# Token counts in full 128-column weight blocks, and an experts' planner that knows of exposed weight loads

## The chip, the cores and the metric

The kernel runs on one core of a Trainium2 chip. The metric is the time of one execution on the device in microseconds (us), the median of three runs. A profiled execution of the same kernel gives the trace from which all rows below are taken; times in it count from its first instruction. The engines are PE (TensorE, its weight loads shown apart as PEld), DVE (VectorE), ACT (ScalarE), POOL (GpSimd) and SP, which here only issues DMAs.

## What is computed

```python
attn_out = softmax(q @ pooled(k).T / 8) @ pooled(v)    # 8 x 8 heads, 576 tokens, width 64
x = attn_out.transpose(0, 2, 1, 3).reshape(4608, 512)
# mixture of 8 experts, each takes exactly 576 tokens (cap)
flat = (x @ w_gate).flatten()
for idx in np.argsort(-flat):            # best (token, expert) pairs first
    tok, e = idx // 8, idx % 8
    if assigned[tok] >= 0 or counts[e] >= cap: continue
    assigned[tok] = e; counts[e] += 1
for e in range(8):
    out[assigned == e] = np.maximum(x[assigned == e] @ w1[e], 0) @ w2[e]
# gated feed-forward over all tokens
y = (sigmoid(out @ w_gate2) * (out @ w_val)) @ w_out   # 512 -> 1536 -> 512
```

## The kernel before

There are three stages. Attention and the logits of the gate take the first 155 us of the profile. Then come the experts, and last the gated feed-forward, whose loads and splits begin under the experts' last steps.

**The choice of the tokens.** The greedy loop is replaced by eight rounds, k = 0 to 7. In a round each token that is still free has a key, its best open logit, in two parts `kh` and `kl`. The round must find the key at which the first expert is full. `search` (L898) does it twice, by 16 bits of the key each time, in four steps of four bits, so a round makes eight counts (the last round makes none). For one count DVE compares all keys with 15 thresholds into `C` (128 partitions x 36 token columns x 32, of which 15 are used), PE multiplies `C` as weights with `EoU` (which expert each token wants) and adds up in PSUM (`rps`, in round 0 `acc0`), DVE compares the count with the free places (`hit`, with `fl` as its sum), and PE multiplies `fl` with a table `trw`, which gives the next 15 thresholds. Each of these four links waits for the one before it. In round 0 a matmul takes one token column of 15 thresholds, so a count is 36 matmuls, and one more (`one16` with `nrem`) subtracts the 576 places. In rounds 1 to 6 a matmul takes three token columns, 79 weight columns (3 x 32, less the 17 unused of the last) against 24 of `EoU`, so a count is 12 matmuls; DVE then adds the three diagonal blocks in `jk`, by one subtraction of `rem` and two additions.

After the eight counts a round goes on with `EG` and `tot` (which expert is full), then `est`, the expert's number. From there SP may load that expert's weights (`load`, L1062: four of 1 MB into `stg`); in this document that moment is "the expert is chosen". Then `before`, `inc`, `OHH`, `OHL` and `R` make the list `idxs` of the 576 tokens (36 matmuls `rps<-R,OHL`), after which POOL gathers the tokens' rows by indirect DMAs (`xg`), and the round is "done".

**The experts.** Expert k is computed in two halves of 288 tokens (u), each in eight steps f, so 128 steps of 24 products: 12 for `hps` (g_h, L1198) and 12 for `acc` (g_o, two steps behind). The products are float32 split in a high and a low part: `xh`, `xl`, `hh`, `hl` and the weights `w`, split from `stg` by ACT (high) and DVE or POOL (low). DVE makes `hl` and `xl` from PSUM after ACT has made `hh` and `xh`. The gathered tokens are turned by PE (`hps<-identf,xg`, three transposes to a `turn`, four turns to a half). DVE and ACT also convert the last stage's weights (`cx`, `cs`, `cw`), 36 tiles of four DVE instructions.

**What sets the order.** Rounds 1 to 7 run between the products of earlier experts. `experts` (L1048) is a planner in Python that issues instructions while `Clock` (L634) models the time of each engine; `note` (L678) has the cost of each instruction, 0.039 us for a small matmul with over 64 weight columns. Between groups of three products, `groups` comes back to the loop at L1290: `fill` (L1182) puts in turns, splits and conversions whose data are ready and whose engine is free by the model, and `route` (L1119) goes one link on in the round when that link's data are ready by the model or will be before the next products can run. Every instruction goes through one helper, so that nearly all rows of the experts show L628.

Of the kernel before, what the change touches and what calls it, by code (L numbers as in the profile page):

```python
# [8 lines left out]
F32R = mybir.dt.float32r  # L9
# [4 lines left out]
OP = mybir.AluOpType  # L14
# [8 lines left out]
CAP = N // E  # L23
F1 = 1024
F2 = 1536
NT = N // 128
# [607 lines left out]
class Clock:  # L634
    HOP = 0.15

    def __init__(self, nc):
        self.nc = nc
        self.t = {n: 0.0 for n in ("tensor", "vector", "scalar", "gpsimd", "sync", "dma")}
        for n in ("tensor", "vector", "scalar", "gpsimd", "sync"):  # L640
            setattr(self, n, Lane(self, getattr(nc, n), n))
        self.spans, self.rings, self.free = {}, {}, {}
        self.held = {"vector": deque(maxlen=64), "gpsimd": deque(maxlen=64)}
# [34 lines left out]
    def note(self, lane, op, args, kw):  # L678
# [5 lines left out]
        t = self.t  # L684
# [10 lines left out]
        if "dma" in op:  # L695
            big = max([a.nbytes() for a in aps], default=0)
            t[lane] = start + (1.03 if lane == "gpsimd" else 0.5)
            first = max(t["dma"], t[lane] + 0.8)
            t["dma"] = first + big / 360e3
            end = t["dma"] + 1.0  # L700
        else:
            if lane == "tensor":
                n = aps[-1].free_size() if op == "matmul" else aps[1].partition_size() * 2
                n *= 4 if op == "matmul" and aps[-1].dtype == F32 else 1
                cost = max(0.039 if op == "matmul" and aps[1].free_size() > 64 else 0.0245, n / 2400 + 0.013)
            elif lane == "vector":
                wide = op == "tensor_tensor" and all(mybir.dt.size(a.dtype) == 2 for a in aps)
                cost = 0.069 + n / (1920 if wide else 960)
            elif lane == "scalar":
                cost = 0.07 + n / 1200  # L710
            elif lane == "gpsimd":
                cost = 0.15 + n * 0.0021
            else:
                cost = 0.3
            end = t[lane] = start + cost
            if alone:
                self.held[lane].append((start, end))
# [10 lines left out]
class Router:  # L728
# [168 lines left out]

    def search(self, k, key, w):  # L898
        nc, C, EoU = self.nc, self.C, self.EoU
        g, parts = (1, 3) if k == 0 else (3, 1)  # L900
        TR = self.tr0[:, w]
        for i in range(4):
            if i or w:
                for c in range(0, NT, NT // parts):
                    cs = slice(c, c + NT // parts)
                    nc.vector.tensor_tensor(C[:, cs, 0:15], key[:, cs, None].to_broadcast([128, NT // parts, 15]),
                                            TR[:, None, :].to_broadcast([128, NT // parts, 15]), op=OP.is_ge)
                yield 0.8 / g, (C[:, 0:NT // parts],)
            if k:
                cp = self.psum.tile([32 * g, g, E], F32, name="rps", bufs=1)  # L910
            else:
                cp = self.spare.tile([128, UA], F32, name="acc0", bufs=1)[0:32, 0:E].rearrange("p (g e) -> p g e", g=1)
            for c in range(NT // g):
                nc.tensor.matmul(cp[0:32 * g - 17], C[:, g * c:g * c + g].rearrange("p c t -> p (c t)")[:, 0:32 * g - 17],
                                 EoU[:, g * c:g * c + g], start=c == 0, stop=c == NT // g - 1, skip_group_check=True)
                if c == 0 and not k:
                    nc.tensor.matmul(cp[0:15, 0], self.one16[:, 0:15], self.nrem, start=False, stop=False, skip_group_check=True)
            hits = cp[0:15, 0]
            if k:
                hits = self.jk  # L920
# [1 line left out]
                for j in range(g - 1):  # L922
                    nc.vector.tensor_tensor(hits, cp[32 * j:32 * j + 15, j], hits, op=OP.add)
            rows = slice(32 * i, 32 * i + 15)
            nc.vector.tensor_scalar(self.hit[rows], hits, 0.0, None, op0=OP.is_ge, op1=OP.max, accum_out=self.fl[rows])
            yield 0.05, (self.fl,)
            TR = self.psum.tile([128, 15], F32, name="rps", bufs=1)
            nc.tensor.matmul(TR, self.fl.to_broadcast([128, 128]), self.trw[:, w, i], start=True, stop=True)
# [119 lines left out]
def experts(tc, c, w, xio, psum, router, conv, xD, w1, w2, x2D, ahead, spare):  # L1048
    nc = router.nc
    ident = c["ident"]  # L1050
    now = nc.t
    with ExitStack() as ctx:
# [4 lines left out]
        steps = [(k, u, f) for k in range(E) for u in range(2) for f in range(8)]  # L1057
        order = [(half, which) for half in range(2) for which in range(2)]
        splits, turns, lows, banks = deque(), deque(), deque(), []
        st = {"chosen": 0, "phase": 0, "load": 0, "split": 0, "gather": 0, "turn": 0, "h": 0, "o": 0, "gap": False, "ahead": False}  # L1060

        def load(k, half, which):  # L1062
            eng = nc.gpsimd if (k, half) == (0, 1) else nc.sync
# [96 lines left out]
        def do_turn(force=False):  # L1160
            t = turns[0]
            if force or (st["h"] >= 8 * (2 * t[0] + t[1]) - 8 and len(lows) < 3 and nc.idle(banks[-3]) <= now["tensor"] and nc.when([xg[t[0], t[1], 2]]) <= now["tensor"]
                         and now["scalar"] <= now["tensor"] + 0.3):
                do_lows(1)
                turn(*turns.popleft())
                return True
# [15 lines left out]
        def fill():  # L1182
            do_lows()
            late = False
            while st["gap"] and turns and (turns[0][0], turns[0][1], 2) in xg:
                if not do_turn():
                    late = st["h"] >= 8 * (2 * turns[0][0] + turns[0][1]) - 4 and nc.when([xg[turns[0][0], turns[0][1], 2]]) <= now["tensor"] + 1.0
                    break
# [100 lines left out]
        heat(nc.when([xT[0, 0][0][:, 0]]))  # L1289
        for need in groups():  # L1290
            fill()
            while wait["on"] and (wait["ready"] <= now["tensor"] + 0.05 or wait["ready"] < nc.when(need) - 0.1):
                route()
                fill()
        assert not splits and not turns and not lows


# [751 lines left out]
```

## Time and profile before

| | |
|---|---|
| median of 3 runs | 1486.81 us (1486.62 to 1488.14) |
| the profiled execution's own time | 1487.1 us |
| span of its instructions | 1485.4 us |
| PE busy | 1443.0 us, 97% of the span |
| DVE busy | 1199.4 us, 81% |
| ACT, POOL busy | 578.4 and 453.9 us |
[...]

The profiled execution took 1.7 us more than its span, and 0.3 us more than the median. Busy shares are over all stages; below they are read by stage.

### The profile page before, as it was taken

The page shows a single profiled execution, that of the slowest core. Times are in us where ns is not written, and L with a number is a line of the kernel's source. Part 1 is how long each engine was busy: PE and PEld are TensorE (multiplying, and loading weights), DVE is VectorE, ACT ScalarE, POOL GpSimd, SP SyncE. Part 2 cuts the span into 40 slices and gives each one's busy share as a digit, 9 for nine tenths or more (in the row PEclk, how much of TensorE's full clock was granted, in tenths as well). Part 3 has the DMA queues.
Part 4 walks back from the last instruction along what each step waited for, and adds up shares of the span by engine and source line. Part 5 has one row for each costly group of instructions (what it writes and reads, how often), then busy time and mean ns, then how long its engine had stood idle before and what let it go on. Part 6 is the DMA issues. An engine that isn't in the chain of part 4 may idle for free.

```text
span 1485.4 us, 29007 instructions
## 1 busy us (share of the span) xinstructions
PE 1443.0 (97%) x11228; PEld 1323.7 (89%) x11228; DVE 1199.4 (81%) x2590; ACT 578.4 (39%) x1138; POOL 453.9 (31%) x461
## 2 busy tenths in 40 slices
PE   8999699999999999999999999999999999999997
PEld 6888489999999999998888888888888899999996
DVE  6889788988899987578788868888787897887884
ACT  5665143343433434445434333323432233333321
POOL 5682042254334412202234311112211231334221
PEclk9999699999999999999999999999999999999998
DMA  9994346545554776676565664554756377766751
GB/s 334 315 312 134 104 148 204 174 128 205 189 172 147 225 252 199 249 270 236 213 234 183 231 266 177 216 204 173 259 189 243 135 255 270 284 239 243 297 222 70
DMA packets 133130, 319.25 MB, mean 215 GB/s; under 512 B 13724, under 2 KB 55232, under 8 KB 118784
## 3 DMA queue, kind: packets, MB, share of 16 engines
q1 hardware_dynamic: 125428, 295.39, 56.1%
q0 software_dynamic: 6496, 20.98, 4.2%
q8 instruction: 89, 1.46, 0.4%
q10 hardware_dynamic: 1068, 1.03, 0.3%
q14 instruction: 49, 0.40, 0.1%
HBM read 240.42 MB, written 72.89 MB: 211 GB/s over the span
## 4 chain that ended last, share of the span: by engine, by line
PE 84%; DVE 9%; issue 2%; DMA 2%; ACT 1%; POOL 1%; SPq 1%; ACTq 0%; POOLq 0%; DVEq 0%
PE hps L628 12%; PE acc L628 12%; PE pj L1812 11%; PE Yg L1645 7%; PE Yv L1645 7%; PE pj L1859 7%; PE Zg L1645 5%; PE Xg L1645 5%; PE Zv L1645 5%; PE Xv L1645 5%; PE aps L530 2%; PE rps L628 2%; DVE cx L628 1%; PE sps L469 1%; PE qps L505 1%
## 5 line engine op out<-in xcount | busy, mean ns | idle before, releaser
L628 PE MATMUL acc<-hh,w 128*128 128x288 f32 x1024 | 244.9, 304 | 0.0
L628 PE MATMUL hps<-xh,w 128*128 128x288 f32 x1024 | 234.5, 300 | 1.2 <-DVE hl L628 1.1
L628 PEld LDWEIGHTS acc<-hh,w 128*128 128x128 f32 x1024 | 176.3, 189 | 0.2
L628 PEld LDWEIGHTS hps<-xh,w 128*128 128x128 f32 x1024 | 174.1, 188 | 2.3 <-DVE hl L628 1.8
L628 PE MATMUL acc<-hl,w 128*128 128x288 f32 x512 | 151.1, 295 | 0.9 <-DVE hl L628 0.9
L628 PE MATMUL hps<-xl,w 128*128 128x288 f32 x512 | 151.3, 296 | 0.1
L628 ACT ACTIVATE hh<-hps 128x288 fp32r<-128x288 f32 x128 | 52.5, 410 | 234.6 <-PE hps L628 219.4
L628 POOL TENSOR_TENSOR w<-stg,w 128x512 fp32r<-128x512 f32 x76 | 107.9, 1433 | 114.7 <-ACT w L628 108.6
L1829 DVE TENSOR_TENSOR stg<-pj,stg 128x512 f32<-128x512 f32 (+1 forms) x196 | 121.5, 627 | 23.7 <-PE pj L1812 17.7
L1645 PE MATMUL Yg<-w 128*128 128x512 f32 (+1 forms) x540 | 126.4, 369 | 0.0
L1645 PE MATMUL Yv<-w 128*128 128x512 f32 (+1 forms) x540 | 125.6, 367 | 0.0
L1711 ACT ACTIVATE sg<-sg 128x512 f32<-128x512 f32 (+1 forms) x90 | 53.0, 589 | 177.8 <-DVE sg L1682 110.9
L628 POOL DMA_INDIRECT xg<-x_rows,idxs x48 | 46.2, 963 | 223.0 <-PE hps L628 70.9
L1645 PEld LDWEIGHTS Yv<-w 128*128 128x128 f32 x540 | 98.7, 188 | 13.0 <-DVE vc L1681 0.3
L1645 PEld LDWEIGHTS Yg<-w 128*128 128x128 f32 x540 | 95.8, 189 | 11.4
L628 PEld LDWEIGHTS acc<-hl,w 128*128 128x128 f32 x512 | 96.7, 189 | 1.1 <-DVE hl L628 1.1
L628 PEld LDWEIGHTS hps<-xl,w 128*128 128x128 f32 x512 | 96.4, 188 | 0.3 <-DVE xl L628 0.3
L628 ACT ACTIVATE w<-stg 128x512 fp32r<-128x512 f32 (+1 forms) x137 | 80.8, 639 | 35.4 <-DVE capv L628 29.9
L1645 PE MATMUL Xg<-w 128*128 128x512 f32 (+1 forms) x360 | 84.4, 369 | 0.5 <-ACT cw L628 0.5
L1645 PE MATMUL Zg<-w 128*128 128x512 f32 (+1 forms) x360 | 84.4, 369 | 0.2 <-DVE sg L1689 0.2
L1645 PE MATMUL Zv<-w 128*128 128x512 f32 (+1 forms) x360 | 84.2, 369 | 0.0
L1645 PE MATMUL Xv<-w 128*128 128x512 f32 (+1 forms) x360 | 83.6, 367 | 0.0
(326 smaller groups left out, 3264.6 us busy)
## 6 DMA issues: line engine op xcount, KB each, us to landing
w<-w_split SPq DMA_DIRECT2D x84, 1024.0 KB
stg<-in_moe_w_dram SPq DMA_DIRECT2D x30, 1024.0 KB
w_split<-w SPq DMA_DIRECT2D x21, 1024.0 KB
woh<-wo_parts SPq DMA_DIRECT2D x38, 512.0 KB
wr<-wo_parts SPq DMA_DIRECT2D x19, 768.0 KB
kv<-in_k_dram SPq DMA_DIRECT2D x12, 768.0 KB
kv<-in_v_dram SPq DMA_DIRECT2D x12, 768.0 KB
x_cols<-x SPq DMA_DIRECT2D x15, 576.0 KB
```

Of the source, the lines that this page charges most:

```text
L469: eng.matmul(p[cs, r, G * j:G * j + G], t.ap[rs, h % 4, cs], kpT[rs, b if b is not None else 4 * n + 2 * c + r, h], start=True, stop=True)
L505: eng.transpose(p[:z, j], flat[:, a:a + z], ident)
L530: eng.matmul(p[:, a + s:a + s + 2], t[:, j + s], flat[:, x0:x1 + 1:x1 - x0], start=a + s == 0, stop=True, skip_group_check=True)
L628: r = f(*args, **kw)
L1645: eng.matmul(t, W(a, k), X(b, k), start=first and n == 0, stop=n == 5, skip_group_check=True)
L1711: x = fl.op(A, lambda eng: eng.activation(T(g), T(g), AF.Sigmoid), after=[op], rank=rank)
L1812: eng.matmul(self.tile(ps)[:, 256 * i:256 * i + 256], G(a), W(b), start=j < 4 and i == 0 and q == 0, stop=True, skip_group_check=True)
L1829: y = fl.op({"vector": 0.15 + n * 256 / 960}, lambda eng: eng.tensor_tensor(A(), P(), A(), op=OP.add), after=[x, st["acc", u, k, t, d]], r ...
L1859: eng.matmul(self.tile(ps), G(a), W(b), start=n == 0, stop=n == 5)
```

## The change

Three things are edited. In `search`, a matmul of rounds 1 to 6 takes four token columns (128 weight columns against 32 of `EoU`), so a count is nine matmuls, and DVE adds four diagonal blocks (one subtraction, three additions). In round 0 a matmul takes all 32 columns of its token, the comparison is made in four pieces of nine token columns instead of three of twelve, and the places are compared with 576 on DVE instead of being subtracted by a matmul. In `Clock.note`, a product (float32 in one pass, `F32R`) that follows anything else on PE costs 0.083 us more. In the planner, a turn is put off while a round is running, unless the planner is about to go on with that round (`near`) or the turn is nearly due; and from round 3 on a link of the round is issued only when by the model its data have been ready for 0.5 us.

```diff
 class Clock
+        self.big = True
...
                 cost = max(0.039 if op == "matmul" and aps[1].free_size() > 64 else 0.0245, n / 2400 + 0.013)
+                big = op == "matmul" and aps[-1].dtype == F32R
+                if big and not self.big:
+                    cost += 0.083
+                self.big = big
...
 def search(self, k, key, w)
-        g, parts = (1, 3) if k == 0 else (3, 1)
+        g, parts = (1, 4) if k == 0 else (4, 1)
...
-                yield 0.8 / g, (C[:, 0:NT // parts],)
+                yield 0.75 if k == 0 else 0.3, (C[:, 0:NT // parts],)
...
             for c in range(NT // g):
-                nc.tensor.matmul(cp[0:32 * g - 17], C[:, g * c:g * c + g].rearrange("p c t -> p (c t)")[:, 0:32 * g - 17],
+                nc.tensor.matmul(cp[0:32 * g], C[:, g * c:g * c + g].rearrange("p c t -> p (c t)"),
                                  EoU[:, g * c:g * c + g], start=c == 0, stop=c == NT // g - 1, skip_group_check=True)
-                if c == 0 and not k:
-                    nc.tensor.matmul(cp[0:15, 0], self.one16[:, 0:15], self.nrem, start=False, stop=False, skip_group_check=True)
...
-            nc.vector.tensor_scalar(self.hit[rows], hits, 0.0, None, op0=OP.is_ge, op1=OP.max, accum_out=self.fl[rows])
+            nc.vector.tensor_scalar(self.hit[rows], hits, 0.0 if k else float(CAP), None, op0=OP.is_ge, op1=OP.max, accum_out=self.fl[rows])
...
 def fill() in experts
             while st["gap"] and turns and (turns[0][0], turns[0][1], 2) in xg:
+                k, u, i = turns[0]
+                if len(banks) < 3 or wait["on"] and not st["near"] and st["h"] < 8 * (2 * k + u) - 4 + i:
+                    break
                 if not do_turn():
...
 the loop at L1290
-            while wait["on"] and (wait["ready"] <= now["tensor"] + 0.05 or wait["ready"] < nc.when(need) - 0.1):
+            while wait["on"] and (wait["ready"] <= now["tensor"] + (0.05 if st["phase"] < 3 else -0.5) or wait["ready"] < nc.when(need) - 0.1):
+                st["near"] = True
                 route()
                 fill()
+            st["near"] = False
```

The order of the instructions that comes out of it follows from the planner, not from the diff alone. The first place is on PE, in a round that runs under the third expert's steps: the end of a count, and what stands there until the next link (`fl`). Before:

```order
L628 LDWEIGHTS C
L628 MATMUL rps<-EoU,C 79x24
L628 MATMUL hps<-xh,w 128x288
L628 MATMUL hps<-xl,w 128x288
L628 MATMUL hps<-xh,w 128x288 x2
L628 MATMUL hps<-xl,w 128x288
L628 MATMUL hps<-xh,w 128x288
L628 MATMUL acc_6220<-hh,w 128x288
L628 MATMUL acc_6220<-hl,w 128x288
L628 MATMUL acc_6220<-hh,w 128x288
L628 LDWEIGHTS fl
L628 MATMUL rps<-trw,fl 128x15
```

Of the change, at a like place:

```order
L628 LDWEIGHTS C
L628 MATMUL rps<-EoU,C 128x32
L628 MATMUL hps<-identf,xg 128x96 x3
L628 MATMUL acc_6111<-hh,w 128x288
L628 MATMUL acc_6111<-hl,w 128x288
L628 MATMUL acc_6111<-hh,w 128x288
L628 MATMUL hps<-xh,w 128x288
L628 MATMUL hps<-xl,w 128x288
L628 MATMUL hps<-xh,w 128x288 x2
L628 MATMUL hps<-xl,w 128x288
L628 MATMUL hps<-xh,w 128x288 x2
L628 MATMUL hps<-xl,w 128x288
```

The last of nine matmuls instead of twelve is shown; a turn now follows the count at once, and more products (15 instead of 9) stand before the next link. Over the experts' stage the order has 576 count matmuls before and 432 now, the same 3072 products and 180 transposes, and the returns from anything else to a product fall from 158 to 149.

The second place is on DVE, between a count and its threshold in round 1 (`jk` adds the blocks, `hit` decides). Before:

```order
L628 TENSOR_TENSOR C<-kh,rps 128x36x15
L628 TENSOR_TENSOR w<-stg,w 128x512
L628 TENSOR_TENSOR jk<-rps,rem 15x8
L628 TENSOR_TENSOR jk<-rps,jk 15x8 x2
L628 TENSOR_SCALAR hit,fl<-jk 15x8
L628 SCALAR_TENSOR_TENSOR cx<-cw,cx 128x512
```

Of the change:

```order
L628 SCALAR_TENSOR_TENSOR cx<-cs,cx 128x512
L628 SCALAR_TENSOR_TENSOR hl<-hps,hh 128x288
L628 TENSOR_TENSOR xl<-hps,xh 128x288
L628 TENSOR_TENSOR jk<-rps,rem 15x8
L628 TENSOR_TENSOR jk<-rps,jk 15x8 x3
L628 TENSOR_SCALAR hit,fl<-jk 15x8
```

One more addition stands in each of the 48 counts of rounds 1 to 6. The rounds also come to their ends later. By the products ahead of each round's list of tokens, rounds 1 to 7 are done at step 11.8, 23.8, 36.6, 49.4, 62.8, 75.8 and 79.8 before, and at 11.5, 24.6, 40.6, 56.2, 72.2, 86.6 and 90.2 now, while expert k's products begin at step 16k in both. The order of the gated stage is unchanged on PE.

## Rows read from the trace of the kernel before

**Rows 1.** The page's head and first part: busy us, share of span.
```profile
span 1485.4 us, 29007 instructions
```

**Rows 2.** Windows by stage: us, then busy time by engine, PEclk, DMA share, GB/s.
```profile
155.00:195.00 40.00, 28.41 (x441) 17.61 (x441) 26.76 (x126) 6.43 (x13) 6.05 (x6) 0.66 0.41 133
195.00:560.00 365.00, 358.91 (x3337) 349.44 (x3338) 322.98 (x956) 148.58 (x324) 131.97 (x107) 1.00 0.56 185
672.80:1485.40 812.60, 801.28 (x4420) 718.57 (x4419) 644.19 (x984) 274.57 (x480) 208.46 (x184) 1.00 0.60 220
```

**Rows 3.** Waits of PE, 195 to 345 us (rounds 1 to 3): us in total, times, longest.
```profile
PE rps L628 <- DVE C L628: 1.5, 1, 1.5
PE hps L628 <- DMA xg<-x_rows,idxs: 0.6, 1, 0.6
```

**Rows 4.** Waits of PE, 345 to 672.8 us (the later rounds and steps).
```profile
PE hps L628 <- DVE hl L628: 1.5, 4, 0.5
PE rps L628 <- DVE EG L628: 0.9, 1, 0.9
PE acc L628 <- DVE hl L628: 0.9, 1, 0.9
PE rps L628 <- DVE hit L628: 0.4, 1, 0.4
PE rps L628 <- DVE EoU L628: 0.2, 1, 0.2
```

**Rows 5.** Timeline of PE, one count: start us, us, what.
```profile
256.77 0.61 PE L628 MATMUL rps<-EoU,C 128*79 128x24 bf16 x12
257.23 0.38 PE L628 MATMUL acc<-hh,w 128*128 128x288 f32 x1
257.45 0.29 PE L628 MATMUL acc<-hl,w 128*128 128x288 f32 x1
```

**Rows 6.** Timeline of PE, three small matmuls with 128 weight columns.
```profile
283.97 0.20 PE L628 MATMUL rps<-rs,before 128*128 128x1 bf16 x2
284.03 0.16 PE L628 MATMUL rps<-rs,onesb 128*128 128x1 bf16 x1
284.06 0.38 PE L628 MATMUL acc<-hh,w 128*128 128x288 f32 x1
```

**Rows 7.** Weight loads by form, 195 to 510 us: busy us, mean ns.
```profile
L628 PEld LDWEIGHTS <-C 128*79 128x79 bf16 x576 | 29.1, 124 | 3.2 <-DVE C L628 1.7 <-DVE EoU L628 0.4 <-issue 0.2
L628 PEld LDWEIGHTS <-fl 128*128 128x128 bf16 x48 | 4.6, 96 | 3.8 <-DVE hit L628 0.6
```

**Rows 8.** Timeline of round 0, DVE and PE.
```profile
157.31 0.30 DVE L890 TENSOR_TENSOR C<-kh,tr 128x150 bf16<-128x150 f32 x1
...
163.85 0.85 DVE L628 TENSOR_TENSOR C<-kh,rps 128x180 bf16<-128x180 f32 x3 [0.29 <-PE rps L628]
...
164.31 1.02 PE L628 MATMUL acc<-EoU,C 128*15 128x8 bf16 x35
```

**Rows 9.** Timeline of PE, 36 matmuls with 32 weight columns.
```profile
185.08 1.07 PE L628 MATMUL rps<-R,OHL 128*32 128x36 bf16 x36 [0.37 <-DVE OHL L628]
```

**Rows 10.** Timeline of DVE, the additions after a count.
```profile
271.95 0.16 DVE L628 TENSOR_TENSOR jk<-rps,rem 15x8 f32<-15x8 f32 x1
272.14 0.34 DVE L628 TENSOR_TENSOR jk<-rps,jk 15x8 f32<-15x8 f32 x2
```

**Rows 11.** Timeline of DVE and POOL just ahead of the longest wait.
```profile
258.32 3.15 DVE L628 SCALAR_TENSOR_TENSOR cx<-cs,cx 128x512 f32<-128x512 f32 x1
258.36 2.54 POOL L628 TENSOR_TENSOR w<-stg,w 128x512 fp32r<-128x512 f32 x2
```

**Rows 12.** Timeline of round 3: the expert's weights, from choice to first split.
```profile
333.77 0.13 DVE L628 TENSOR_SCALAR est<-m 1x1 int32<-1x1 f32 x1
334.74 2.35 SPq L628 DMA_DIRECT2D stg<-in_moe_w_dram  x4
...
341.12 0.62 ACT L628 ACTIVATE w<-stg 128x512 fp32r<-128x512 f32 x1
```

More of the change, by code (lines that the diff above doesn't have):

```diff
@@ L1059, in experts @@
         splits, turns, lows, banks = deque(), deque(), deque(), []
-        st = {"chosen": 0, "phase": 0, "load": 0, "split": 0, "gather": 0, "turn": 0, "h": 0, "o": 0, "gap": False, "ahead": False}
+        st = {"chosen": 0, "phase": 0, "load": 0, "split": 0, "gather": 0, "turn": 0, "h": 0, "o": 0, "gap": False, "ahead": False, "near": False}
         def load(k, half, which):
```

## The prediction

> **What bounds the kernel now.** I read the page's head first, for the span that the sum is made against: 1485.4 us [rows 1], with 1.7 us around it in the profiled execution (1487.1 us), which is 0.3 us above the median. Then the windows by stage, to see which engine sets each [rows 2]. From 155 to 195 us no engine is full (PE 28 of 40 us) and the granted clock averages 0.66: this is round 0, where DVE and PE wait for each other in turn, so every link counts in full. From 195 to 560 us, where rounds 1 to 7 run under the products, PE is busy 358.9 of 365 us: PE is the bound, and what it is relieved of comes off the time. DVE is next with 323.0 us, 88%. The gated stage has PE busy for 801 of 813 us; its order on PE is untouched, so it starts when the experts end and lasts as long as before. Third, the waits of PE [rows 3, 4]: seven groups, 6.0 us in all, six of them for DVE. That is all that a better order can give by removing waits. The rest of a gain must come from work that PE no longer does.
>
> **The counts of rounds 1 to 6.** Now twelve matmuls with 79 weight columns run from 256.77 to 257.23 us, 0.46 us or 0.038 each [rows 5]. Neither 24 nor 32 moving columns can be what takes that time: three matmuls with one moving column take 0.09 us [rows 6], so it is the loads or the issue. What do nine with 128 columns take? No count with 128 columns is in the trace, so I bound it. From above: the next row in weight columns below it, 79, has 0.038 each, and a load no faster than that gives nine x 0.0385 = 0.35 us. From below: the three with 128 columns [rows 6] take 0.06 for the first two and 0.03 for the third, so nine take about 0.06 + 7 x 0.027 = 0.25 us. I take 0.25, because those rows have the same weight columns and type, and because a load of 128 bf16 columns takes 96 ns against 124 ns for one of 79 [rows 7]: the full block is the faster load, not the slower. Saved: 48 counts x (0.46 - 0.25) = 10.1 us; with the upper bound 48 x (0.46 - 0.35) = 5.3 us.
>
> [...]
>
> **Returns to a product.** The first product after a count shows 0.38 us where the next has 0.29 [rows 5]: its load lies open for 0.09 us. The order has nine returns fewer (158 to 149): 9 x 0.09 = 0.8 us. The turn that now stands behind a count costs the same three transposes as before, and the new 0.083 in the planner's costs is no time by itself; it only moves links.
>
> **Round 0.** Its counts wait for the first piece of the comparison. Three pieces of 180 elements take 0.85 us together and one of 150 alone takes 0.30 [rows 8]; between these, an element costs at most 0.55 / 390 = 0.0014 us. A first piece of 135 instead of 180 should end up to 0.06 us sooner; I take 0.045, seven times (the first count's comparison is made elsewhere): 0.3 us. The last piece still lands before the matmuls reach it: four pieces, at the 0.28 us that each of the three takes, are done by 1.13 us, and the 28th matmul comes some 0.35 + 27 x 0.029 = 1.13 us after the start. One matmul fewer in each of eight counts, at 1.02 / 35 = 0.029 us [rows 8], is 0.2 us. Against it stand 32 instead of 15 weight columns. 36 such matmuls take 1.07 us, 0.030 each [rows 9], the same as 0.029, but rows 8 were taken at a lower clock. From above I bound them by the 0.038 of 79 columns, 36 x 8 x 0.009 = 2.6 us. I take nothing, as 15 and 32 columns come out alike. Round 0: -0.5 us, between -0.5 and +2.1. It is hidden by nothing, since the experts' first products wait for its list.
>
> **DVE's added work.** One more `jk` in each of 48 counts; the next one starts 0.19 us after the one before [rows 10]: 9.1 us in 48 pieces. Its place is 195 to 560 us, where DVE would be busy 323.0 + 9.1 = 332 us of some 354, 94% instead of 88. In a link the addition lengthens the chain by 0.19 us and the shorter count takes 0.21 off, so the threshold comes as early as before. Queued behind it are `hl` and `xl`, for which PE waits already, 2.4 us [rows 4]. How much of the crowding reaches PE no row shows. Below: nothing, as DVE's idle time is still 22 us. Above: half of the 9.1 us, when every second addition pushes an `hl` that is needed at once. I take 2 us, nearer the lower end, because in the 365 us PE waited for `hl` in five places only.
>
> **The planner's order.** From round 3 on a link waits 0.5 us longer by the model. Three waits there are of links [rows 4]: EG 0.9, hit 0.4, EoU 0.2. 0.5 us off each leaves 0.4: -1.1 us. The longest wait (C, 1.5 us) is earlier [rows 3], in round 2, where the rule does not apply. It came from a conversion that took 3.15 us because POOL split weights beside it [rows 11]. The change keeps such pairs, so one like it stays likely. Since a turn is put off and a round takes more products, rounds 3 to 7 are done 4 to 11 steps later, and expert k's weights are asked for later. What covers that: expert 3's four loads are issued at 334.74 us and its first split runs at 341.12, 7.4 us after the choice [rows 12]. In the new order round 3 is done at step 40.6 and is chosen before that, while the products of expert 3 start at step 48. Seven steps of 24 products at 0.13 us (0.22 from the first to the second, less the open 0.09 [rows 5]) are 22 us. I cost it at nothing; the cover is gone once a choice comes some 15 us later than planned, and then each late us is a us of PE.
>
> **The sum.** Counts -10.1, returns -0.8, round 0 -0.5, links' waits -1.1, DVE +2.0: -10.5 us. Against the profiled 1487.1 that gives 1476.6, and against the median, 0.3 lower, **1476.3 us**, a ratio of 0.993.
>
> **The rivals.**
>
> 1. A load of 128 columns in a count is no faster than one of 79 (0.0385 each). For it: the planner's own costs know only one value over 64 columns, and such loads stand only in short runs [rows 6]. Against it: the shorter load [rows 7]. The gain on counts is 5.3 instead of 10.1 us: 1481.1 us.
> 2. DVE gives half of its added work on to PE and the links' waits move instead of going, as `hl` waits: +4.5 instead of +2.0, and 0 instead of -1.1. For it: six of seven wait groups are already for DVE, and at 94% the slack is thin. Against it: DVE has some 42 idle us in the stretch now [rows 2], and PE waited for it 5.4 us in all [rows 3, 4]. 1479.9 us; if all 9.1 us came through, 1484.5.
> 3. Slower: a load takes time in proportion to its columns, 0.0385 x 128 / 79 = 0.062 us. Nine take 0.56 us, 0.10 more than now, +4.8 us on 48 counts, and with the other terms (-0.8, -0.5, -1.1, +2.0) the kernel takes 1491.2 us. It decides as soon as a matmul with 128 columns takes over 0.052 us, where nine equal the present count. Against it stand [rows 6, 7].
> 4. Also slower: the later rounds bring weights or tokens late. It decides when the five experts of rounds 3 to 7 wait together for over 10.5 us, about 2.1 us each; with 4 us each the kernel takes 1476.3 + 20 = 1496.3 us. Against it: the 15 us of cover.
> 5. Nothing comes of it: PE's gain is waited away at the seam to the gated stage, where weights must be there. For it: DMAs are busy 0.60 of the gated stage [rows 2]. Against it: the gated stage's loads are issued by steps, so they move with PE. 1486.8 us.
>
> **How the numbers follow.** A measurement of this kernel tells about 0.2%, 3 us, from no change, so faster is below 1483.8 us. My forecast, 1472 to 1479 us by itself, has 0.62; rival 1 0.13; rival 2 0.14; rivals 3 and 4 together 0.05; rival 5 0.06. Downward the range takes in a planner that removes most of the waits (4 us more than I count), 1472; upward rivals 1 and 2, to 1482.5. Faster: 0.62 + 0.13 + 0.12 = 0.87; same: 0.02 of rival 2 and 0.06 of rival 5, 0.08; slower 0.05.
>
> **What would show it.** In the new profile a count should read x9 with about 0.25 us from its start to the next product; 0.35 there means rival 1, over 0.46 rival 3. Loads of `C` should show some 96 ns instead of 124. The last product of the experts should end near 662 us instead of 672.8. Waits of PE for `hl` and `xl` over 5 us in sum mean rival 2, waits for DMAs or for ACT's `w` at steps 48, 64, 80 or 96 rival 4, a wait ahead of the first gated product of over 1 us rival 5. The prediction is wrong above all if the matmul's pitch in a count is not that of [rows 6].

## The result, and the profile after

The changed kernel takes 1494.9 us (median of 5, 1492.6 to 1496.1) where the kernel before takes 1487.6 on the same chip: a ratio of 1.0052, 95% interval 1.0041 to 1.0064. It is slower by half a per cent, where 0.7% faster was forecast. The profiled execution took 1492.64 us with a span of 1490.8 us, 5.4 more than before [rows 1]; it is the fastest of the five, 2.3 us under their median, so that what is read from it below explains 5.4 of the 7.3 us.

First the windows by stage, with the columns of [rows 2] (busy us by engine, granted clock, DMA share, GB/s):

```profile
195.00:560.00 365.00, 349.37 (x3171) 336.59 (x3172) 330.32 (x1000) 144.70 (x319) 133.24 (x107) 0.99 0.54 180
678.40:1490.80 812.40, 801.14 (x4419) 718.66 (x4419) 644.98 (x985) 274.59 (x480) 208.68 (x184) 1.00 0.60 220
```

The gated stage is as long as before (812.4 against 812.6 us). The loss is between 195 and 678 us. There PE is busy 9.5 us less in the same 365 us, so it does not work more: it stands. The granted clock also shows 0.99 instead of 1.00. Next the counts, in PE's timeline (start us, us, what):

```profile
488.52 0.39 PE L628 MATMUL rps<-EoU,C 128*128 128x32 bf16 x9
488.76 0.45 PE L628 MATMUL hps<-identf,xg 96*128 96x96 f32 x3
```

A count now takes 0.24 us until the next matmul, against 0.46 [rows 5]: 48 x 0.22 = 10.6 us of PE's time are gone, as forecast. Why then is the stage longer? The waits of PE, 195 to 345 us and 345 to 678.4 us (us in total, times, longest):

```profile
PE rps L628 <- DVE C L628: 3.4, 2, 2.2
PE rps L628 <- DVE hit L628: 2.5, 2, 1.3
PE rps L628 <- DVE EG L628: 0.2, 1, 0.2
...
PE rps L628 <- DVE hit L628: 5.5, 1, 5.5
PE rps L628 <- DVE OHL L628: 2.4, 2, 1.5
PE hps L628 <- DMA xg<-x_rows,idxs: 2.1, 4, 0.9
PE hps L628 <- DVE hl L628: 0.3, 1, 0.3
```

Against [rows 3, 4] the waits for links of a round (`C`, `hit`, `OHL`, `EG`, `EoU`) have grown from 3.0 to 14.0 us, and one wait for a `hit` is 5.5 us long. All groups of the waits added up, from 190 to 690 us, give 18.2 us, against 7.3 before; this sum is called "the waits" below. (It takes in 0.5 us at the seam to the gated stage in nearly every kernel, and 0.8 to 1.4 us for tokens, `acc<-xg`, ahead of the experts' first product; inside the experts' stage alone it is 16.4 against 5.9 us.) What happens at the longest one is in the timeline of DVE, POOL and PE:

```profile
491.59 0.92 POOL L628 DMA_INDIRECT xg<-x_rows,idxs  x1 [0.31 <-issue]
492.20 0.68 DVE L628 TENSOR_TENSOR w<-stg,w 128x512 fp32r<-128x512 f32 x1
...
492.82 0.92 POOL L628 DMA_INDIRECT xg<-x_rows,idxs  x1 [0.30 <-PE rps L628]
493.17 6.09 DVE L628 SCALAR_TENSOR_TENSOR cx<-cs,cx 128x512 f32<-128x512 f32 x1
493.76 4.94 POOL L628 TENSOR_TENSOR w<-stg,w 128x512 fp32r<-128x512 f32 x4
499.29 0.17 DVE L628 TENSOR_TENSOR jk<-rps,rem 15x8 f32<-15x8 f32 x1
...
500.29 0.20 PE L628 MATMUL rps<-trw,fl 128*128 128x15 bf16 x1 [5.46 <-DVE hit L628]
500.34 0.59 PE L628 MATMUL acc<-hh,w 128*128 128x288 f32 x1
500.72 0.44 PE L628 MATMUL acc<-hl,w 128*128 128x288 f32 x1
```

A conversion `cx`, 0.67 us elsewhere, takes 6.09 us: it begins while a gather runs on POOL, four splits stand behind the gather, and the conversion ends 0.56 us after the fourth split. Behind it on DVE stand `jk` and `hit`, for which PE waits. The products after the wait start 0.24 us apart (500.72, and 500.96 in the next row) where elsewhere they are 0.13 apart. The windows give the granted clock there and at a second place:

```profile
499.30:506.10 6.80, 5.81 (x32) 5.67 (x33) 3.37 (x13) 0.66 (x1) 0.00 (x0) 0.50 0.40 116
506.20:513.00 6.80, 6.80 (x61) 6.65 (x60) 5.41 (x18) 4.82 (x11) 2.89 (x2) 1.00 0.00 1
550.40:553.90 3.50, 3.50 (x19) 3.47 (x18) 2.16 (x5) 1.61 (x4) 0.00 (x0) 0.52 0.64 243
```

For 6.8 us, the last 1.0 us of that wait among them, PE runs at a granted clock of 0.50 instead of 1.00 and gets through 32 matmuls where the next 6.8 us have 61. The second stretch, 3.4 us, follows two waits for `OHL` (1.5 us the longer). They stand at the end of a DVE queue without a pause, in which an `sl` took 3.12 instead of 0.19 us in the same company, a gather and two splits, and `R`, `OHL` and a `cx` behind it took about 1 us more each, beside single splits. Before, no wait was longer than 1.5 us and the clock stayed at 1.00.

So the account of the experts' stage, from the first product to the last (194.9 to 672.8 us before, 195.7 to 678.4 now, 4.8 us more): counts -10.6, returns -0.8, waits inside the stage +10.5 (16.4 less 5.9), and half of the 9.3 us at half clock that lie outside the waits, +4.6, give +3.7. The account stays 1.1 us short, more than the returns come to. The remaining 0.8 us of the span is a later start of the stage, which moves by as much from kernel to kernel here.

### The profile page after: what moved, and what is told of

The parts are those of the page before. It is cut to its first block, busy times and chain, and to the rows that moved or that the text cites. A ratio compares the mean times of both kernels' runs of the same rounds, so it can differ in the third digit from the quotient of the medians.

```text
span 1490.8 us, 28744 instructions
## 1 busy us (share of the span) xinstructions
PE 1437.3 (96%) x11073; PEld 1314.3 (88%) x11076; DVE 1210.0 (81%) x2642; ACT 577.3 (39%) x1138; POOL 459.9 (31%) x464
## 3 DMA queue, kind: packets, MB, share of 16 engines
q1 hardware_dynamic: 125428, 295.39, 56.2%
q10 hardware_dynamic: 1068, 1.03, 0.3%
## 4 chain that ended last, share of the span: by engine, by line
PE 84%; DVE 8%; DMA 4%; issue 2%; ACT 1%; POOL 1%; SPq 1%; POOLq 0%; ACTq 0%; DVEq 0%
PE hps L628 13%; PE acc L628 12%; PE pj L1820 11%; PE Yg L1653 7%; PE Yv L1653 7%; PE pj L1867 7%; PE Zg L1653 5%; PE Xg L1653 5%; PE Zv L1653 5%; PE Xv L1653 5%; DMA kv<-in_v_dram 2%; PE aps L530 2%; PE rps L628 2%; DVE cx L628 1%; DMA xg<-x_rows,idxs 1%
## 5 line engine op out<-in xcount | busy, mean ns | idle before, releaser
L628 POOL TENSOR_TENSOR w<-stg,w 128x512 fp32r<-128x512 f32 x78 | 111.0, 1439 | 94.1 <-ACT w L628 86.9
```

Of the source, the lines that this page charges most:

```text
L628: r = f(*args, **kw)
```

## The experiments

Three theories went into the first four experiments. **Shut-out:** the loss is made by DVE instructions that are held for a whole run of POOL's splits, and by the half clock after it. **Late rounds:** the rounds, and with them weights and tokens, come too late. **Crowding:** the additions of the new counts leave DVE no room. From no_slack on the question is where such waits come from: from the planner's new rules, the put-off of turns above all (**put-off**, also A and P), or from the chance of the one order (**luck**, also B and R).

**1. swap_four: the changed kernel, four splits moved.** Only the four splits of the rows above go from POOL to DVE; the planner is not told, so the order on PE stays.

```diff
 def split(k, half, which, j, lane)
-            getattr(nc, lane).tensor_tensor(lo[:, j], s[:, j], hi[:, j].bitcast(F32), op=OP.subtract)
+            if (k, half, which, j) in [(5, 1, 0, x) for x in range(4)]:
+                nc.nc.vector.tensor_tensor(lo[:, j], s[:, j], hi[:, j].bitcast(F32), op=OP.subtract)
+                nc.note(lane, "tensor_tensor", (lo[:, j], s[:, j], hi[:, j].bitcast(F32)), {"op": OP.subtract})
+            else:
+                getattr(nc, lane).tensor_tensor(lo[:, j], s[:, j], hi[:, j].bitcast(F32), op=OP.subtract)
```

> The changed kernel with one thing moved: the four low-part splits of expert 5's second half of w1, which POOL ran without a pause behind three gathers at 493.8 to 498.7 us, are issued on DVE at the same places; the planner is not told, so every other instruction keeps its place. Theory shut-out (DVE cannot get at its operands while POOL works without a pause behind a gather; the 5.5 us wait and the half clock after it come from that one pile-up): the 6.09 us conversion falls to under 1 us, PE's 5.5 us wait and the slow products after it go, about 7 us less than the changed kernel, 1486 to 1489 us. Theory late rounds (the rounds, and with them weights and tokens, come too late around steps 72 to 96, whoever splits): the wait stays under another name, under 2 us gained, 1493 us or more. Theory crowding (DVE has no room left): 2.7 us more on DVE make it slower, 1495 us or more.

Measured: 1486.5 us against 1487.5, ratio 0.9993 (0.9983 to 1.0003). The same conversion in DVE's timeline, and what follows it:

```profile
494.44 0.68 DVE L628 SCALAR_TENSOR_TENSOR cx<-cs,cx 128x512 f32<-128x512 f32 x1
495.15 0.17 DVE L628 TENSOR_TENSOR jk<-rps,rem 15x8 f32<-15x8 f32 x1
```

It takes 0.68 us, the 5.5 us wait and the 6.8 us at half clock are gone, and with them the whole loss, although DVE has four instructions more. That the loss hangs on this one run of splits is shown; late rounds forecast under 2 us of gain here, and crowding a loss. Its size is less firm: 0.0059 of the time, some 9 us, between two ratios taken on different chips (1.0052 and 0.9993), but 5.4 us between the spans of the two profiled executions (1490.8 and 1485.4). Waits of 14.3 us and 3.4 us at half clock remain, so it is not all.

**2. swap_two: only the last two of the four moved.** Does the length of the run count? The list in the edit above is (5, 1, 0, 2) and (5, 1, 0, 3).

> As the kernel with four splits moved, but only the last two of the four go to DVE; POOL still runs two behind the gathers. Theory shut-out: a DVE instruction that begins under a gather waits for the whole run behind it, 2.5 us for two splits (2.48, 2.93 and 2.45 us in three places so far), 3.9 for three, 5.4 for four. So the conversion is stretched by 2.5 us instead of 5.4, PE's wait falls from 5.5 to about 2.5 us and the granted clock stays up or falls for a shorter time: 1487 to 1491 us, between the changed kernel and the one with four moved. Rival (the wait is due to something else at that place, such as late splits): no proportion, 1486 or 1493 us.

Measured: 1490.5 us against 1490.8 on this chip, ratio 0.9992 (0.9979 to 1.0004). DVE, POOL and PE in the timeline:

```profile
494.57 0.92 POOL L628 DMA_INDIRECT xg<-x_rows,idxs  x1 [0.30 <-issue]
494.94 3.64 DVE L628 SCALAR_TENSOR_TENSOR cx<-cs,cx 128x512 f32<-128x512 f32 x1
495.50 2.52 POOL L628 TENSOR_TENSOR w<-stg,w 128x512 fp32r<-128x512 f32 x2
...
499.61 0.18 PE L628 MATMUL rps<-trw,fl 128*128 128x15 bf16 x1 [3.01 <-DVE hit L628]
```

With two splits the same conversion takes 3.64 us, 2.97 more than alone, and PE's wait is 3.0 instead of 5.5 us. The hold and the wait follow the run. The time did not do so: it was expected between the changed kernel and swap_four, and its ratio is that of swap_four, although 3.0 us of wait are left. In the profiled execution the experts' stage is 482.9 us long, as long as in the changed kernel (482.7), because four stretches of 3.4 us ran at half clock. Two of them:

```profile
213.91:217.32 3.41, 3.41 (x16) 3.26 (x16) 2.26 (x11) 0.41 (x1) 0.00 (x0) 0.50 0.77 213
323.13:326.54 3.41, 3.41 (x23) 3.41 (x21) 2.48 (x10) 0.77 (x2) 0.00 (x0) 0.50 0.02 5
```

They follow waits of 1.2 and 2.2 us. The changed kernel, whose order is the same there, has the same two waits and stayed at full clock behind them. So what a wait costs behind it is not settled by the order, and the half-clock term of one profiled execution need not be that of the next.

**3 and 4. The change in its two halves.** counts_only has the edits in `search` alone, planner_only the edits in `Clock` and the planner alone.

> The kernel before with the edits of the counts alone (four token columns in rounds 1 to 6, 32 columns and four pieces in round 0); the planner and its costs as before, so it places the nine matmuls by its own old rules. PE's work falls by 11 us as in the whole change. Theory shut-out: the loss of the whole change is a pile-up that its order happens to have, so this order keeps most of the 11 us unless it has a pile-up of its own: 1477 to 1483 us, and a wait of more than 3 us would stand behind a conversion stretched beside POOL. Theory late rounds: here rounds are done at steps 39.6, 53.8, 67.6, 81.8, earlier than in the whole change, so 1479 us or less. Theory crowding (the added additions on DVE eat the gain): 1486 us or more.

> The changed kernel with the counts as before (three token columns, 79 weight columns; round 0 as before): the new cost of an open load, the put-off turns and the 0.5 us alone. PE's work falls by 1.1 us (144 returns instead of 158). Theory shut-out: same as before within 5 us to either side, depending on pile-ups: 1482 to 1492 us. Theory late rounds: slower, 1490 to 1497 us, since rounds are done at 38.2, 52.5, 66.6, 81.2. Theory crowding: 1486 us, since DVE has no added work.

Measured: counts_only 1488.2 us, ratio 1.0004 (0.9996 to 1.0013), planner_only 1492.6 us, 1.0033 (1.0020 to 1.0045). The counts alone gain nothing either: the old rules, given the shorter counts, wrote another order, with waits of 12.8 us and 17 us at half clock (15.1 of them outside the waits). DVE and POOL of counts_only at its longest stretch:

```profile
518.58 0.92 POOL L628 DMA_INDIRECT xg<-x_rows,idxs  x1 [0.30 <-issue]
519.01 6.12 DVE L628 SCALAR_TENSOR_TENSOR cx<-cw,cx 128x512 int32<-128x512 int32 x1
519.53 5.03 POOL L628 TENSOR_TENSOR w<-stg,w 128x512 fp32r<-128x512 f32 x4
```

and of planner_only, with three splits:

```profile
468.99 0.92 POOL L628 DMA_INDIRECT xg<-x_rows,idxs  x1 [0.30 <-PE rps L628]
469.66 4.59 DVE L628 SCALAR_TENSOR_TENSOR cx<-cw,cx 128x512 int32<-128x512 int32 x1
469.94 3.75 POOL L628 TENSOR_TENSOR w<-stg,w 128x512 fp32r<-128x512 f32 x3
```

The stage is 2.8 us longer than before in counts_only: -10.6 for the counts, +5.8 for the waits inside it, +7.5 for the half clock give +2.7. The counts' gain is there and is lost again, in an order that the new rules had no part in. Late rounds had forecast 1479 us or less for it. Its time is the one that crowding forecast (1486 us or more), and that of planner_only the one that late rounds forecast (1490 or more); the next run has both the late rounds and the additions.

**5. no_deferral: the changed kernel without the put-off of turns.**

```diff
 def fill() in experts
-                k, u, i = turns[0]
-                if len(banks) < 3 or wait["on"] and not st["near"] and st["h"] < 8 * (2 * k + u) - 4 + i:
-                    break
```

> The changed kernel without the rule that puts off a turn while a round runs; the rest of the change stays. Turns and gathers come as early as before, rounds are done at 40.2, 55.6, 71.6, 87.4, as late as in the whole change; 164 returns instead of 149 cost 1.2 us. Theory shut-out: gathers stand elsewhere among POOL's splits, so the 5.5 us wait at step 78 goes or moves; 1478 to 1490 us, with the waits again behind conversions beside POOL. Theory late rounds: 1492 us or more, as the rounds are as late. Theory crowding: 1490 us or more.

Measured: 1477.7 us against 1487.5, ratio 0.9931 (0.9918 to 0.9944): close to what was forecast for the changed kernel (0.993). The waits of PE in its experts' stage:

```profile
PE hps L628 <- DMA xg<-x_rows,idxs: 2.6, 3, 1.3
PE rps L628 <- DVE hit L628: 2.0, 1, 2.0
PE hps L628 <- DVE hl L628: 0.3, 1, 0.3
```

In all 6.6 us, and 3.4 us at half clock. With waits like those of before, the counts' gain comes through: the stage is 469.5 us long, 8.4 less than before. By the planner its rounds are as late as in the changed kernel, and the additions are in it, so late rounds (1492 us or more) and crowding (1490 or more) are out. Is the put-off the culprit, then, or is this just a lucky order?

**6 and 7. no_slack and no_open_load: the changed kernel without one of the two other rules** (0.05 for every round in the loop at L1290; `cost += 0.0`). One execution each.

> The changed kernel without the 0.5 us that a link is held back from round 3 on. Theory put-off (turns that are put off bring the gathers, and with them tokens and splits, into one knot): deferral is still in, so 1484 us or more, with waits for gathered tokens of 3 us or more. Theory luck (each order has its own pile-ups, and the rules do not matter on average): anywhere from 1472 to 1496 us. If the 0.5 us does what it is for, waits for links (C, hit, EG, OHL) grow by some us against the changed kernel apart from the pile-up at step 78.

> The changed kernel with 0 instead of 0.083 us for an open load in the planner's costs. Theory put-off: 1484 us or more, as turns are still put off. Theory luck: anywhere from 1472 to 1496 us. In both, the waits of 3 us or more stand behind a DVE instruction that begins under a gather with two or more splits behind it, or behind a gather's tokens.

Measured: 1493.5 and 1499.9 us, with 1490.8 for the kernel before; waits 18.5 and 18.4 us. Taking either rule away leaves the waits. Without the slack they are spread (`hit` eight times, 5.5 us in all, 1.3 the longest); only one DVE instruction of the rounds was held for a run of splits, by 1.9 us, and the rest by single splits. The links' waits are 14.1 us there, against 8.5 in the changed kernel without its longest one, so the slack does shorten them. The 1499.9 us of no_open_load lie outside what luck allowed (1472 to 1496). It also began the experts' products 4 us later than the changed kernel, at 200.0 us.

**8. nd_fifteen: no_deferral with 15 columns in round 0.** In `search`, `cp[0:32 * g if k else 15]` and the same for `C`.

> The changed kernel without the put-off turns, and with 15 instead of 32 weight columns in round 0's matmuls; four pieces and no subtracting matmul as in the change. If 32 columns cost 0.003 us more for each matmul (1.12 us for 36 in the changed profile against 1.02 for 35), a count of round 0 falls from 1.97 to some 1.87 us; if the columns cost nothing there, it stays at 1.97. Round 0 ends 0.7 us sooner; the whole, 1476 to 1478 us, can't tell that from nothing.

Measured in one execution: 1476.8 us, span 1474.8. It is the order of no_deferral on every engine, so only round 0 differs; see the point on round 0 below.

**9 and 10. after_070 and nd_070: 0.070 instead of 0.083**, in the changed kernel and in no_deferral: nothing that an engine does changes in kind, but the planner writes another order.

> The changed kernel with one number of the planner different: 0.070 instead of 0.083 us for the first product after a small matmul. Nothing that the engines do is changed in kind; only where links and turns fall. Theory A, the put-off of turns is what brings the waits, whatever the order: PE waits of 10 to 17 us in the experts' stage again, as in all five kernels with the put-off so far, and 1484 to 1496 us. Theory B, it is chance of the one order (which conversion falls under which POOL run): the time lies anywhere between 1475 and 1496 us, with the waits between 5 and 17 us, and the size of the waits follows from the longest conversion beside a gather and its splits: under 1480 us if no DVE instruction is stretched by more than 2.4 us.

> The changed kernel without the put-off of turns, with 0.070 instead of 0.083 us in the planner for the first product after a small matmul. Theory A, without the put-off waits stay near 6 us: 1475 to 1481 us. Theory B, chance of the order: anywhere from 1475 to 1496 us, again after the longest stretched DVE instruction: over 1484 us only where one is stretched by 3.9 us or more under a gather with three or more splits.

Measured in one execution each: 1481.6 and 1486.1 us, with 1491.8 for the kernel before; waits 10.3 and 13.8 us. With the put-off the kernel gained 0.7%, without it 0.4%: the theory that the put-off decides is out in that form, as far as single executions tell. DVE and POOL of after_070, at its two longest stretches:

```profile
429.01 0.92 POOL L628 DMA_INDIRECT xg<-x_rows,idxs  x1 [0.30 <-PE rps L628]
429.40 6.11 DVE L628 TENSOR_TENSOR C<-kl,tr 128x540 bf16<-128x540 f32 x1
429.95 4.96 POOL L628 TENSOR_TENSOR w<-stg,w 128x512 fp32r<-128x512 f32 x4
...
526.05 5.03 POOL L628 TENSOR_TENSOR w<-stg,w 128x512 fp32r<-128x512 f32 x4
526.14 5.17 DVE L628 SCALAR_TENSOR_TENSOR inc<-inc,base,M 128x36 f32<-128x36 f32 x2
```

Two DVE instructions were held for four splits each, and yet PE waited only 3.4 us for the first, and no link that follows `inc` waited over 0.7 us. In nd_070 no DVE instruction of these rounds was held by more than 2.4 us, and it took over 1484 us, by many waits of 1.7 us or less. So the expectation that the longest stretch sets the time failed too. A shut-out seems to cost what is queued behind it and needed at once, less the products that still stand ready; this reading was not tested by itself.

**11 and 12. after_hold and nd_hold: a planner that is told.** A gather costs 1.23 instead of 1.03 us in `note` and its span is added to the times in which DVE cannot run (`self.held[lane].append((start, t[lane]))`).

> The changed kernel, put-off included, with a planner that counts a gather of POOL as holding DVE off (1.23 us). Theory A, the put-off brings the waits by itself: 10 us of PE waits or more, 1484 us or more. Theory C, the put-off only places work under gathers that the planner believed free: with gathers counted the waits fall under 7 us and the time is 1474 to 1481 us.

> The changed kernel without the put-off of turns, with a planner that also counts a gather of POOL as holding DVE off (1.23 us, on the list of times in which DVE's instructions can't run), as it does for splits. If the runs of a gather and splits behind it are what stretch DVE's instructions, the planner now sees them and keeps DVE's needed instructions out of most: no PE wait over 2 us in the experts' stage, under 6 us in sum, 1473 to 1479 us. If the planner's times are too far from the chip's for that (the order on each engine is fixed, the moments are not), it gives the 1477.7 us of the kernel without the put-off, or a chance value between 1476 and 1490 us.

Measured: 1499.3 us each, for nd_hold a ratio of 1.0050 (1.0036 to 1.0064); waits 16.0 and 18.8 us, the largest group 4.8 and 7.7 us for gathered tokens (`xg`). Neither stays under the 1490 us that nd_hold was to reach at most. In each two DVE instructions were still held for whole runs (by 2.6 and 4.2 us in after_hold, 2.9 and 2.4 in nd_hold), and 20.5 and 17.1 us ran at half clock. Why the tokens came late was not followed up. A model that was meant to be righter in one place did not write a better order.

**13 to 15. Other orders: before_v1, before_v2, nd_090.** The kernel before with 0.072 instead of 0.069 (DVE's fixed cost), the kernel before with 0.037 instead of 0.039 (wide matmuls), and no_deferral with 0.090 instead of 0.083, all in `note`.

> The kernel before, of which nothing is changed but one number of its planner: 0.072 instead of 0.069 us for the fixed part of a DVE instruction. No edit of the change is in it. Theory R, any new order that this planner writes waits more than the order of before, which is the lucky one: PE waits of 9 to 18 us in the experts' stage instead of 6, and a ratio to before of 1.002 to 1.009. Theory P, the waits come from the changed planner's rules (the put-off above all): waits of 5 to 8 us, and a ratio of 0.998 to 1.002.

> The kernel before with another number of its planner moved: 0.037 instead of 0.039 us for a matmul with over 64 weight columns. As for the one beside it: theory R, PE waits of 9 to 18 us in the experts' stage and 3 to 13 us more than before; theory P, waits of 5 to 8 us and within 3 us of before.

> The changed kernel without the put-off of turns, with 0.090 instead of 0.083 us for the first product after a small matmul. Theory R: waits between 6 and 18 us by chance, so the time is 0.992 to 1.004 of before, and stage length = work of PE + waits + half of the time at half clock again, within 4 us. Theory P: without the put-off the waits stay at 5 to 8 us and the time at 0.992 to 0.995 of before.

Measured: before_v1 1488.5 us against 1488.4, ratio 0.9999 (0.9988 to 1.0011), waits 8.0 us; before_v2 in one execution 1495.4 us, 7 us more than before, waits 14.5 us; nd_090 in one execution 1480.9 us, waits 9.5 us. The largest group of before_v2, 345 to 681 us:

```profile
PE hps L628 <- DVE hl L628: 6.8, 2, 5.9
```

A planner's cost that is off by 0.002 us, with nothing of the change in it, lost as much as the change did, by a wait for an `hl` and with no gather near. Ahead of that `hl` on DVE stood the first links of a new round, three of them held by about 1 us each beside a run of three splits, and 6.8 us ran at half clock. One redrawn order in two was as good as the order of before.

**16. best: the kernel of 8, timed.**

> The changed kernel without the put-off of turns and with 15 instead of 32 weight columns in the counts of round 0. Its order on every engine is that of the kernel without the put-off, so its waits should be the same 5.6 us, and each of eight counts 0.07 us shorter: 0.5 us less than that kernel's ratio of 0.9931 gives, 0.9928 of before (0.991 to 0.994).

Measured: 1478.3 us against 1488.4, ratio 0.9930 (0.9917 to 0.9944), waits 7.5 us. It beats the kernel before by 0.7% and the changed kernel by 1.2% (0.9930 / 1.0052 = 0.988). It is not told apart from no_deferral (0.9931); the 0.6 us between them in round 0 is less than these intervals.

All orders side by side, by waits: with the put-off 10.3, 12.0, 16.0, 18.2, 18.4 and 18.5 us; the changed planner without it 6.6, 9.5, 13.8 and 18.8; the old rules 7.3, 8.0, 12.8 and 14.5. The groups overlap. That the put-off makes long waits likelier is possible and not settled by so few; that an order drawn anew by this planner carries 7 to 18 us of waits is shown.

## Why the prediction was wrong

**The failed step is "The planner's order".** It priced the new order at -1.1 us, by taking 0.5 us off each wait of before, as if the other waits would stay where they were. In the new order one stayed: the wait for `C` at 262 us, 1.3 us now, behind a conversion held by 1.9 us. The others are new. In the stage the waits grew by 10.5 us and brought 4.6 us of half clock, which had no term at all. The step even named the cause ("one like it stays likely", of the conversion beside two splits [rows 11]) and left it at the 1.5 us that it had cost; it did not ask what the same pair costs when the run is four splits long and a `hit` is queued behind it. Splits stand behind gathers on POOL in both kernels, and which of them run back to back, with what on DVE beside them, depends on the moment, which the order of the instructions alone does not tell. Why the planner's model missed it is not shown: telling it of the gathers did not help (after_hold, nd_hold).

**The counts** were right: 0.24 us by forecast 0.25, and the loads of `C` in the weight loads by form, 195 to 510 us, as in [rows 7]:

```profile
L628 PEld LDWEIGHTS <-C 128*128 128x128 bf16 x405 | 13.2, 96 | 7.6 <-DVE C L628 4.4
```

96 ns for 128 columns against 124 for 79: rivals 1 and 3 are out.

**Returns**: nine fewer, 0.8 us, less than the 1.1 us by which the account above stays short, so no run shows this gain.

**Round 0** was put at -0.5 us and gave nothing. Its matmuls in PE's timeline, before:

```profile
163.62 0.20 PE L628 MATMUL rps<-trw,fl 128*128 128x15 bf16 x1 [0.36 <-DVE hit L628]
165.59 0.20 PE L628 MATMUL rps<-trw,fl 128*128 128x15 bf16 x1 [0.26 <-DVE hit L628]
```

the changed kernel:

```profile
163.73 0.19 PE L628 MATMUL rps<-trw,fl 128*128 128x15 bf16 x1 [0.36 <-DVE hit L628]
164.31 1.12 PE L628 MATMUL acc<-EoU,C 128*32 128x8 bf16 x36 [0.39 <-DVE C L628]
165.69 0.19 PE L628 MATMUL rps<-trw,fl 128*128 128x15 bf16 x1 [0.26 <-DVE hit L628]
```

then the kernel best, with 15 columns:

```profile
163.35 0.19 PE L628 MATMUL rps<-trw,fl 128*128 128x15 bf16 x1 [0.36 <-DVE hit L628]
163.94 1.05 PE L628 MATMUL acc<-EoU,C 128*15 128x8 bf16 x36 [0.39 <-DVE C L628]
165.25 0.20 PE L628 MATMUL rps<-trw,fl 128*128 128x15 bf16 x1 [0.26 <-DVE hit L628]
```

From one `fl` matmul to the next a count takes 1.96 us in the changed kernel and 1.90 with 15 columns; before it was 1.97. The 32 columns were costed at nothing because 36 matmuls with 32 took 1.07 us [rows 9] and 35 with 15 took 1.02 [rows 8]; side by side it is 1.12 against 1.05 for 36 each. That is 0.07 a count, 0.6 us in eight, which eats what the smaller pieces and the missing matmul give.

**DVE's crowding** was put at +2.0 us by way of `hl` and `xl`. PE waited 0.3 us for `hl` and not at all for `xl`, less than before. Rival 2 is out in the form that it was given, as waits for `hl`. The additions can be covered: no_deferral and best have them too, and their waits, 6.6 and 7.5 us, are like the 7.3 of before.

**Rivals 4 and 5.** For tokens (`xg`) PE waited 2.1 us as `hps` and 1.4 as `acc`, for the experts' weights not at all, and the first gated product waits the same 0.5 us for `cw`. Neither happened. The slower outcome had a chance of 0.05, all of it on these mechanisms and on rival 3; the one that came was on none of the lists.

## What to carry to other kernels

Where a planner or a scheduler writes the order, any edit to its costs or its inputs redraws the order, and the order that is in the kernel now is one that turned out well: price the gain on the work apart from the waits, and for the waits take what other orders of the same planner have, not the waits of the present one. So test such a change on several orders (a cost moved by a few per cent), and keep the best: 13 orders here lay between 0.993 and 1.006 of the time before, seven of them by a single execution, with the work differing by 0.7%. And read a long PE wait one engine further back: what DVE was held by is in POOL's rows.

## What the runs showed of the hardware

**A DVE instruction can be held for a whole run of POOL's instructions, not for one.** Those that were held so had started under a gather with splits queued behind it, or soon after the start of the first split; the extra time was 2.5 us for two splits [rows 11], 2.97 (swap_two), 3.9 for three (planner_only: 4.59 less 0.67), 5.4 for four (the changed kernel, counts_only and the `C` of after_070), 4.8 for the `inc` of after_070 (5.17 less 0.42). The end of a split, with another queued behind it, need not let DVE in: in the changed kernel the conversion that began at 493.17 us ran on past the ends of three of the four splits and ended at 499.26, 0.56 us after the fourth. It was not so every time: in the kernel before a `C` that began at 395.76 us, under a gather with two splits right behind it, took its 0.72 us. A gather with no split behind it held nothing (the `w` at 492.20 us took its 0.68 us beside one). Inside runs many DVE instructions were held by a single split: this `OHL`, 0.44 us elsewhere, takes 1.1 us more beside two.

```profile
544.94 2.93 POOL L628 TENSOR_TENSOR w<-stg,w 128x512 fp32r<-128x512 f32 x2 [1.37 <-ACT w L628]
545.22 1.52 DVE L628 TENSOR_TENSOR OHL<-slb,iolo 128x576 bf16<-128x576 bf16 x1
```

What decides between the two was not found.

**What reads PSUM was not held.** In the changed kernel 73 DVE instructions with an input in PSUM (`rps`, `hps`), where PE's sums stand, ran beside POOL's runs of two splits or more, and none took over 0.05 us more than its like at the shortest; of the 71 others 33 took over 0.15 us more. An `xl` at its usual 0.46 us and a conversion at 1.82 instead of 0.67, beside five splits:

```profile
202.18 7.10 POOL L628 TENSOR_TENSOR w<-stg,w 128x512 fp32r<-128x512 f32 x5 [3.78 <-ACT w L628]
207.62 0.46 DVE L628 TENSOR_TENSOR xl<-hps,xh 128x288 fp32r<-128x288 f32 x1
208.00 1.82 DVE L628 SCALAR_TENSOR_TENSOR cx<-cw,cx 128x512 int32<-128x512 int32 x1
```

So `jk`, `hl` and `xl` are late by what stands ahead of them on DVE, not by the splits themselves.

**Half clock after a wait.** A wait can cost more than its length: the 5.5 us wait was followed by 5.9 us at a granted clock of 0.50, which is another 2.9 us of products. Stretches of 3.4 or 6.8 us stood in nearly every profiled execution. The three without one (before, nd_070, nd_fifteen) had no wait over 1.7 us; but nd_090, with none over 1.4, had one of 3.4 us, and swap_two and the changed kernel differ behind equal waits of 1.2 and 2.2 us. So the length of the wait does not settle it.
